# Cached attention and a gated MLP in one decode kernel: each 8 MB pair loaded as two halves, one from SyncE's queue and one from ScalarE's

## The chip, the cores and the metric

The kernel runs on one core of a Trainium2 chip. The metric is the device time of one execution in microseconds, the median of the runs shown. A core has five engines with a queue of instructions each: TensorE (PE in the profile, its weight loads PEld), VectorE (DVE), ScalarE (ACT), GpSimd (POOL) and SyncE (SP). Transfers between HBM and the on-chip memory (SBUF) are issued by an engine's queue and carried out by 16 DMA engines, which belong to none of these.

## The reference

For four sequences with one new token each, the result is `g * a + (1 - g) * b`, where `g` is a sigmoid gate.

```
g = sigmoid((x * gate_w).sum(-1, keepdims=True))         # x: 4 x 1 x 1024
# a: attention over a cache
q = (x @ wq) as 32 heads of 128                          # wq: 1024 x 4096
p = softmax(q . k_cache * 128 ** -0.5)                   # k_cache: 4 x 32 x 8192 x 128
a = (p . v_cache) as 4096 columns @ wo                   # v_cache: the same; wo: 4096 x 1024
# b: an MLP (with one token per sequence the choice by w_r chooses that token)
r = x @ w_r
b = x + sigmoid(r) * ((silu(x @ w_gate) * (x @ w_up)) @ w_down)   # F = 3584
```

All inputs are bf16. The caches are 268 MB each; every byte of them is used once, for one query. All inputs together are 576 MB.

## The kernel before

**Pairs.** A cache is worked through in 32 *pairs*. Pair `d` holds four heads of one sequence: 128 partitions (4 heads x 32) with 64 KB each, 8.39 MB. The constant `RING` is half of that per partition (16384 elements, 32 KB), and `UN` is a quarter (16 KB, over all partitions 2 MB): a *unit*. The weights `wq`, `w_gate` and `w_up` come as one pair each, too (`w_gate` and `w_up` with 56 KB per partition), and `w_down` takes the room of a pair.

**The ring.** All of this lands in one SBUF tile, `flat` ("ring" in the profile), with room for `NU` = 11 units. A list written out by hand, `plan`, gives for every load in turn the unit where it begins and the order in which its four units are used (UP: first to last, DOWN: last to first). A pair whose place is 8 or more does not fit in one piece: its second half lies elsewhere (from unit 0, for the last pair from unit 2). The new pair takes up to three units that are free already, and one or more that the pair in use has just given back.

**Loads.** `load_pair` (L194 to L209) issues the load of a pair on SyncE's queue. Where the pair lies in one piece it is a single DMA with rows of 64 KB (L204); where it does not, or where `cuts` asks for it, it is cut (L209). It is called where the pair's use begins: in `wq_piece`'s place (wq), in `gu_piece` (gate and up), in `k_pair` and in `v_pair`. SyncE's instructions are kept in an order that is not written by hand (`manual_schedule` lists PE, DVE and Pool alone), but it issues nearly nothing but these loads, one after the other. Before each it waits on semaphores until PE has done its last matmul on the units that the load overwrites. The wait is for all units of one DMA together.

**Work on K (`k_pair`).** A unit is turned by two transposes of DVE in place (L511, 128x2048 words each), and each of these is followed by 8 matmuls of PE into the scores `S_ps` (L516). After the eighth pair of a group of eight come maximum, exp (on ScalarE, L545) and a transpose of the weights into `PT`.

**Work on V (`v_pair`).** PE multiplies the weights spread out in `PB` with the units, 16 matmuls per unit (L587) into `o_ps`. ScalarE and GpSimd spread `PT` into `PB` (L568, L570); after every second pair `sum_up` folds `o_ps` into `OS` (ScalarE L613, DVE L617), and `finish` brings that into the heads' output.

**Order.** V runs eight pairs (`LAG`) behind K: wq, gate, K0, K1, up, K2 to K8, V0, K9, V1 and so on to K31, then w_down, V23, and the last eight V pairs. `w_down` (`wd_piece`) is loaded and used between K31 and V23. `wo` (`wo_two`, `wo_block`) comes around and behind the last V pair, in pieces that grow smaller, and ends the kernel: its matmuls (L296), a copy and two small stores, one from SyncE and one from ScalarE, which is the only transfer on ScalarE's queue.

**Start.** `begin_early` moves SyncE's first DMA (the load of wq) ahead of the start barrier. After it SyncE issues three small loads of `x`, `w_r` and `gate_w` (L228 to L230).

Of the kernel before, what the change touches and what calls it, by code (L numbers as in the profile page):

```python
# [112 lines left out]
def kernel(  # L113
# [15 lines left out]
    nc = tc.nc  # L129
    P = 128  # L130
    Bn, Sq, D = A_x.shape
    _, H, Sk, Dh = A_k_cache.shape
    F = B_w_gate.shape[1]
    DT = D // P
    NQ = 4
    QP = P // NQ
    JR = Sk // QP // 2
    CJ = 64
    JT = JR // CJ
    RD = 2 * JT  # L140
    GD = QP // RD
    GH = GD * NQ
    ND = Bn * H // NQ
    LAG = GD
# [8 lines left out]
    RING = JR * Dh  # L153
    UN = RING // 2
# [10 lines left out]
    accp = ctx.enter_context(tc.tile_pool(name="accp", bufs=1, space=PSUM))  # L165
    scores = ctx.enter_context(ExitStack())
    scp = scores.enter_context(tc.tile_pool(name="scp", bufs=1, space=PSUM))
    ctx.enter_context(tc.manual_schedule(engines={mybir.EngineType.PE, mybir.EngineType.DVE, mybir.EngineType.Pool}))
    nc.at_finalize(keep_weights)
    nc.at_finalize(drop_implied)  # L170
    nc.at_finalize(begin_early)
# [19 lines left out]
        tb_turn[0] += 1  # L191
        return t[lo:lo + rows, 0:n] if dtype == BF else t[lo:lo + rows, 0:2 * n].bitcast(dtype)

    def load_pair(src, n, cuts=(1, 1), second=None):  # L194

        place, down = next(plan)
        lo = place * UN
        if second is None:
            second = place * UN + n if place + 4 <= NU else 0
        at = [lo, second]  # L200
        assert second or (n == RING and lo + n == NU * UN and not down)
        halves = [flat[:, x:x + n] for x in at]
        if cuts == (1, 1) and second == lo + n:
            nc.sync.dma_start(out=flat[:, lo:lo + 2 * n], in_=src)  # L204
        else:
            for i, half in enumerate(halves):
                step = n // cuts[i]
                for x in range(0, n, step):
                    nc.sync.dma_start(out=half[:, x:x + step], in_=src[:, i * n + x:i * n + x + step])  # L209
        return halves, list(range(RD))[::-1] if down else list(range(RD))  # L210


    S0 = scp.tile([P, 4, NB], F32, name="S_ps")
# [8 lines left out]
        return b[:, 0:n].rearrange("p (%s) -> p %s" % (" ".join(names), " ".join(names)), **dict(zip(names, shape)))  # L222

    N = H * Dh
    wq_at, _ = load_pair(A_wq.rearrange("(c t) n -> c (t n)", t=DT), DT // 2 * N)
    NX = Bn + 2
    x6 = const.tile([NX, D], BF)
    nc.sync.dma_start(out=x6[0:Bn], in_=x2)  # L228
    nc.sync.dma_start(out=x6[Bn:Bn + 1], in_=B_w_r.rearrange("(o n) -> o n", o=1))
    nc.sync.dma_start(out=x6[Bn + 1:Bn + 2], in_=gate_w.rearrange("(o n) -> o n", o=1))  # L230


    q_ps = S0[:, 0:2]
# [61 lines left out]
    def mm_acc(n, lhsT, rhs, start=False):  # L295
        nc.tensor.matmul(acc(n), lhsT=lhsT, rhs=rhs, start=start, stop=True, skip_group_check=True)  # L296
# [20 lines left out]
            mm_acc(n, dg[:], xf[:, n * NB:(n + 1) * NB])  # L317


    TW = DT // 2  # L320


    FI = FG * FR - 1
    FB = P * FI
    SX = 5
# [19 lines left out]

    def wq_piece():
        x_rows(q_ps, wq_at, N // NB, lambda w, t, i: [(0, FR, w[:, t * N + i * NB:t * N + (i + 1) * NB])])

    def q_done():
        qs = turned(P, 8 * P).rearrange("p (z c d) -> p z c d", z=2, c=4)  # L350
# [10 lines left out]
                             start=True, stop=True)  # L361
        nc.vector.tensor_copy(out=qa[:].rearrange("p e h b -> p e (h b)"), in_=qa_ps)

    def gu_piece(view, w_i):

        ws, _ = load_pair(view.rearrange("(c t) f -> c (t f)", t=DT), TW * F)

        def cols(w, t, i):
            row = w[:, t * F:t * F + FB].rearrange("p (f m) -> p f m", m=FI)
            if i < FG - 1:  # L370
                return [(0, FR, row[:, :, FR * i:FR * i + FR])]
            return [(0, FR - 1, row[:, :, FR * i:FI]), (FR - 1, FR, w[:, t * F + FB:(t + 1) * F])]
        x_rows(o_ps[w_i], ws, FG, cols)

    def h_done():
        h = turned(P, 1024, F32).rearrange("p (z n) -> p z n", z=2)
# [24 lines left out]
            nc.gpsimd.tensor_copy(out=cS[lo:lo + m, 0:n], in_=c12[lo:lo + m, 1:2, :].to_broadcast([m, n, Bn]))  # L401
        nc.vector.tensor_tensor(out=hS[:], in0=hs_ps[0:72], in1=cS[:], op=ALU.mult)

    def wd_piece():
        lo = next(plan)[0] * UN
        assert (FI + SX) * D == 2 * RING and lo + 2 * RING <= NU * UN
        w = flat[:, lo:lo + 2 * RING]
        at = FI * D
        nc.sync.dma_start(out=w[:, 0:at], in_=wdv)
        for u in range(2):  # L410
            nc.sync.dma_start(out=w[32 * u:32 * u + 12, at:at + SX * D], in_=wd_apart[u])
        nc.sync.dma_start(out=w[64:72, at:at + D], in_=wd_rest)
        parts = [(hT[:, i // FR, i % FR, :], w[:, i * D:(i + 1) * D]) for i in range(FI)]
        parts += [(hS[:, v, :], w[0:72, at + v * D:at + (v + 1) * D]) for v in range(SX)]
        for i, (lhsT, rows) in enumerate(parts):
            for n in range(NH):
                mm_acc(n, lhsT, rows[:, n * NB:(n + 1) * NB], start=(i == 0))

    WB = P * FR // Dh
    NWB = H // WB  # L420
# [55 lines left out]
    def flush_late():  # L476
        while late:
            late.pop(0)()

    def heads(d):  # L480
        return divmod(d * NQ, H)

    def kv_view(cache, d):
        b, h0 = heads(d)
        return cache[b, h0:h0 + NQ].rearrange("h (r j) d -> (h r) (j d)", j=2 * JR)

    def spread(d):
        b, h0 = heads(d)
        Z = Zt[d % 2]
# [4 lines left out]
    def k_pair(d):  # L494
        g, t = divmod(d, GD)
        Z = Zt[d % 2]
        if d == 0:
            spread(0)
        if t == 0:
            S_ps[g] = S0  # L500
        sps = S_ps[g]
        ks, order = load_pair(kv_view(A_k_cache, d), RING)
        flush_sums()
        for k, n in enumerate(order):
            unit = ks[n // JT][:, (n % JT) * UN:(n % JT + 1) * UN]
            kn = unit.bitcast(U32).rearrange("p (j h i) -> p h j i", j=CJ, h=2)
            T = unit.rearrange("p (j h i e) -> p h j i e", j=CJ, h=2, e=2)
            s = QP - 1 - (RD * t + n)
            for half in range(2):
                step = 2 * k + half  # L510
                nc.vector.transpose(out=kn[:, half], in_=kn[:, half])  # L511
                if step < 2 and ahead:
                    ahead.pop(0)()
                for e in range(2):
                    for z in range(4):
                        nc.tensor.matmul(sps[:, z, :], lhsT=Z[:, 2 * half + e, s:s + P], rhs=T[:, half, 16 * z:16 * z + 16, :, e],  # L516
                                         start=(t + k + half + e == 0),
                                         stop=(t == GD - 1 and k == RD - 1 and half + e == 2))
                if step == RD and d + 1 < ND:
                    spread(d + 1)  # L520
                if step == RD:
                    flush()
                if step == RD + 2:
                    flush_late()
        if t == GD - 1:
            ahead.extend(softmax(g))
            while g > 0 and ahead:
                ahead.pop(0)()
# [45 lines left out]
    def v_pair(d):  # L574
        b, h0 = heads(d)
        g, t = divmod(d, GD)
        tv = t % GV
        row = NM * tv
        flush_sums()
        vv = kv_view(A_v_cache, d)  # L580
        vs, order = load_pair(vv, RING, {ND - 2: (1, 2), ND - 1: (2, 2)}.get(d, (1, 1)), 2 * UN if d == ND - 1 else None)
        for u in range(4 * RD):
            n, z = order[u // 4], u % 4
            vn = vs[n // JT]
            for w in range(4):
                j0 = CJ * (n % JT) + 16 * z + 4 * w
                nc.tensor.matmul(o_ps[w // 2][row:row + NM, w % 2, :],  # L587
                                 lhsT=PB[:, RD * (d % NW) + n, z].rearrange("p w s j -> p (w s j)"),
                                 rhs=vn[:, j0 * Dh:(j0 + 4) * Dh], start=(u == 0), stop=(u == 4 * RD - 1),
                                 skip_group_check=True)  # L590
            if u == 1:
                flush()
            if u == 7:
                flush_late()
        if tv == GV - 1:
            sum_up(d, g, t, b, h0)

        if g == NG - 1:
            if t < 2:
                spread_p(d + NW)  # L600
            if t == 3:
                spread_p(d + NW - 1, 2)
        elif t == NW - 1:
            spread_p(d + 1, NW)
        elif t == GD - 1:
            if g + 1 < NG - 1:
                spread_p(d + 1, NW)
            else:
                spread_p(d + NW)
# [41 lines left out]
    wq_piece()  # L651
    q_done()
    gates()
    gu_piece(B_w_gate, 0)
    side = {1: lambda: (gu_piece(B_w_up, 1), h_done())}
    GE = NWB - HV // WB
    order = []
    for d in range(ND):
# [2 lines left out]
    for kind, d in order:  # L661
        if kind == "k":
            k_pair(d)
            if d in side:
                side[d]()
            if d == ND - 1:
                scores.close()
                fin = ctx.enter_context(tc.tile_pool(name="fin", bufs=1, space=PSUM))
                A_ps.extend(fin.tile([P, NB], F32, name=f"acc{n}") for n in range(NH))
                A_ps.append(fin.tile([P, 2, NB], F32, name="led"))  # L670
                wd_piece()
                add_x()
        if (kind, d) == ("v", ND - 1):
            first, second = wo_two(0)
            first()
            last = [second]
        if kind == "v":
            v_pair(d)
        if (kind, d) == ("v", ND - 2):
            o_rows(0, GE)  # L680
# [47 lines left out]
```

## Time and profile before

| | us |
|---|---|
| median of 3 runs (lowest, highest) | 1341.18 (1341.12, 1342.13) |
| the profiled execution | 1340.96 |
| its span, first to last instruction | 1339.2 |
| PE busy | 1031.3 (77%) |
| DVE busy | 638.7 (48%) |
| POOL busy | 67.0 (5%) |
| ACT busy | 57.7 (4%) |

The page states the busy time of each engine, digits for 40 slices of the span, the DMA queues with what they moved, the chain of work that ended last, and the groups of instructions by line. In the DMA rows a packet is one contiguous row that one DMA engine moves; q1 is SyncE's queue, q10 ScalarE's, q8 and q14 fetch instructions and tables. In the chain in order of time a row has its start, its duration and the work; for a DMA the duration runs from its issue to its landing. In the waits of SyncE's queue a row has who waited for whom, the total in us, how often, and the longest.

### The profile page before, as it was taken

Reading aid. Unit: us, or ns where it says so; the run is one execution under the profiler, and the core shown is the slowest. Engines: PE = TensorE matmul, PEld = TensorE weight load, DVE = VectorE, ACT = ScalarE, POOL = GpSimd, SP = SyncE. Lnnn points to the kernel's source line nnn. Section 1 sums busy time; section 2 is a strip of 40 time slices with the busy share of each in tenths; the row PEclk is TensorE's granted clock in tenths of the full one; section 3 lists DMA queues with packets and bytes.
Section 4 is the critical chain, followed back from the end, with each engine's and each line's share of the span. In section 5 each row is a group of like instructions: output and inputs, shape, how many; then the busy total and the mean of one; then the engine's idle time right before and its main releaser. Section 6 shows DMA issues by size and latency. Waiting matters only on the chain.

```text
span 1339.2 us, 6936 instructions
## 1 busy us (share of the span) xinstructions
PE 1031.3 (77%) x4654; PEld 139.8 (10%) x1486; DVE 638.7 (48%) x385; ACT 57.7 (4%) x58; POOL 67.0 (5%) x174
## 2 busy tenths in 40 slices
PE   2386787887777788777787977777797778687887
PEld 0011000001010010101001110100111011111111
DVE  2285998556553436555352556634345556100001
ACT  0000000100010000100010000100000000110000
POOL 2000000100010000100010000100001000100000
PEclk9697998898888998888889988888998889689999
DMA  9999999999999999999999999999999999999998
GB/s 415 433 437 437 435 437 435 420 438 433 433 435 437 427 433 435 429 438 431 433 431 433 435 439 427 429 433 435 438 430 428 433 429 429 438 429 445 422 422 352
DMA packets 13032, 576.14 MB, mean 430 GB/s; under 512 B 1436, under 2 KB 1700, under 8 KB 1970
## 3 DMA queue, kind: packets, MB, share of 16 engines
q1 hardware_dynamic: 12994, 575.69, 99.6%
q8 instruction: 24, 0.39, 0.1%
q14 instruction: 6, 0.05, 0.0%
q10 hardware_dynamic: 8, 0.00, 0.0%
HBM read 575.68 MB, written 0.01 MB: 430 GB/s over the span
## 4 chain that ended last, share of the span: by engine, by line
DMA 67%; PE 22%; DVE 9%; POOL 0%; ACT 0%; issue 0%; SPq 0%
DMA ring<-in_A_k_cache_dram 53%; PE S_ps L516 15%; DMA ring<-in_A_v_cache_dram 10%; DVE ring L511 9%; PE o_ps L587 5%; DMA ring<-in_B_w_gate_dram 3%; DMA ring<-in_A_wo_dram 2%; PE o_ps L342 1%; POOL PB L570 0%; DVE mx L536 0%; PE led L633 0%; ACT TB L545 0%; PE acc L296 0%; POOL Z L492 0%; PE o_ps L633 0%
## 5 line engine op out<-in xcount | busy, mean ns | idle before, releaser
L511 DVE STREAM_TRANSPOSE ring<-ring 128x2048 uint32<-128x2048 uint32 x256 | 566.5, 2276 | 307.7 <-DMA ring<-in_A_k_cache_dram 307.7
L516 PE MATMUL S_ps<-ring,Z 128*128 128x512 bf16 x2048 | 519.9, 408 | 229.3 <-DVE ring L511 216.1
L587 PE MATMUL o_ps<-ring,PB 128*64 128x512 bf16 x2048 | 457.4, 384 | 35.7 <-DMA ring<-in_A_v_cache_dram 33.3
L516 PEld LDWEIGHTS <-Z 128*128 128x128 bf16 x512 | 53.0, 104 | 683.0 <-issue 683.0
L617 DVE SCALAR_TENSOR_TENSOR OS<-o_ps,mE,OS 128x512 f32<-128x512 f32 x33 | 24.8, 751 | 161.7 <-ACT OS L613 160.2
L587 PEld LDWEIGHTS <-PB 128*64 128x64 bf16 x512 | 56.7, 111 | 428.3 <-issue 427.6
L625 DVE SCALAR_TENSOR_TENSOR OS<-o_ps,mE,OS 128x512 f32<-128x512 f32 x5 | 3.7, 750 | 143.6 <-ACT OS L623 143.6
L492 POOL COPY Z<-qa 32x4 bf16<-32x4 bf16 x128 | 25.8, 201 | 716.7 <-PE S_ps L516 689.6
L570 POOL COPY PB<-PT 32x1024 bf16<-32x1024 bf16 (+3 forms) x23 | 33.4, 1452 | 466.6 <-PE o_ps L587 360.7
L613 ACT ACTIVATE OS<-o_ps,mE 128x512 f32<-128x512 f32 x11 | 7.6, 687 | 671.2 <-PE o_ps L587 671.2
L568 ACT COPY PB<-PT 32x1024 bf16<-32x1024 bf16 (+3 forms) x21 | 30.3, 1444 | 22.4 <-PE o_ps L587 17.4
L545 ACT ACTIVATE TB<-S_ps,mx 128x2048 bf16<-128x2048 f32 x4 | 7.9, 1967 | 321.7 <-DVE mx L542 321.7
L254 PE MATMUL S_ps<-identb,x 6*128 6x6 bf16 x8 | 0.6, 196 | 22.3 <-DMA x<-in_gate_w_dram 22.3
L342 PE MATMUL o_ps<-ring,xw 128*4 128x512 bf16 (+2 forms) x128 | 12.9, 490 | 3.5 <-DMA ring<-in_B_w_gate_dram 3.5
L633 PEld LDWEIGHTS o_ps<-selg,OS 128*128 128x128 f32 x88 | 11.5, 191 | 8.8 <-issue 8.5
L550 DVE STREAM_TRANSPOSE PT<-TB 128x2048 bf16<-128x2048 bf16 x4 | 9.2, 2312 | 6.4 <-ACT TB L545 6.4
L296 PE MATMUL acc<-ring,hT 128*4 128x512 bf16 x54 | 7.9, 466 | 5.5 <-DMA ring<-in_B_w_down_dram 5.5
L536 DVE TENSOR_REDUCE mx<-S_ps 128x1 f32<-128x2048 f32 x4 | 9.1, 2282 | 6.0 <-PE S_ps L516 6.0
L296 PE MATMUL acc<-ring,LT 128*4 128x512 bf16 x64 | 8.8, 378 | 3.3 <-DMA ring<-in_A_wo_dram 2.8
L633 PE MATMUL o_ps<-selg,OS 128*128 128x8 f32 x88 | 10.5, 245 | 0.0
L623 ACT ACTIVATE OS<-o_ps,mE 128x512 f32<-128x512 f32 x5 | 3.4, 687 | 151.2 <-PE o_ps L587 151.2
L256 DVE COPY xw<-S_ps 128x48 bf16<-128x48 bf16 x1 | 0.2, 184 | 17.5 <-PE S_ps L254 17.5
(83 smaller groups left out, 88.4 us busy)
## 6 DMA issues: line engine op xcount, KB each, us to landing
ring<-in_A_v_cache_dram SPq DMA_DIRECT2D x7, 4096.0 KB
ring<-in_A_k_cache_dram SPq DMA_DIRECT2D x6, 4096.0 KB, 33.9
ring<-in_A_v_cache_dram SPq DMA_DIRECT2D x6, 2048.0 KB, 28.9
ring<-in_B_w_gate_dram SPq DMA_DIRECT2D x1, 7168.0 KB
ring<-in_B_w_up_dram SPq DMA_DIRECT2D x1, 7168.0 KB
ring<-in_B_w_down_dram SPq DMA_DIRECT2D x1, 6912.0 KB
ring<-in_A_wo_dram SPq DMA_DIRECT2D x2, 2048.0 KB
ring<-in_A_wo_dram SPq DMA_DIRECT2D x3, 1024.0 KB, 34.5
```

What stands on the lines that cost most here:

```text
L296: nc.tensor.matmul(acc(n), lhsT=lhsT, rhs=rhs, start=start, stop=True, skip_group_check=True)
L342: nc.tensor.matmul(ps[32 * k:32 * k + Bn, z, :].rearrange("p (f r) -> p f r", r=FR)[:, :, lo:hi], lhsT=xT[TW * half + t], rhs=rhs, start=( ...
L492: nc.gpsimd.tensor_copy(out=Z[at, :, QP - 1 + QP * q], in_=qa[at, :, h0 + q, b])
L511: nc.vector.transpose(out=kn[:, half], in_=kn[:, half])
L516: nc.tensor.matmul(sps[:, z, :], lhsT=Z[:, 2 * half + e, s:s + P], rhs=T[:, half, 16 * z:16 * z + 16, :, e], start=(t + k + half + e == 0) ...
L536: nc.vector.tensor_reduce(out=mx[:, 0:1], in_=sps[:].rearrange("p z n -> p (z n)"), axis=AX.X, op=ALU.max)
L550: nc.vector.transpose(out=PT[:].rearrange("p j i -> p (j i)"), in_=PTs)
L568: nc.scalar.copy(out=Bv[at, :, :, q, :], in_=Pv[at])
L570: nc.gpsimd.tensor_copy(out=Bv[at, :, :, q, :], in_=Pv[at])
L587: nc.tensor.matmul(o_ps[w // 2][row:row + NM, w % 2, :], lhsT=PB[:, RD * (d % NW) + n, z].rearrange("p w s j -> p (w s j)"), rhs=vn[:, j0 ...
L617: nc.vector.scalar_tensor_tensor(out=OS[:], in0=o_ps[w // 2][:, w % 2, :], scalar=mE[:, w:w + 1], in1=OS[:], op0=ALU.mult, op1=ALU.add)
L633: nc.tensor.matmul(oT, lhsT=OS[:, q * Dh:(q + 1) * Dh], rhs=selg[:, q].rearrange("p t s -> p (t s)"), start=(q == 0), stop=(q == 3), skip_ ...
```

## The change

`load_pair` is replaced by a list of loads and a function that issues from it:

- `queue` enters a load into `stream`, with its place, its order of use and its four units; all loads are entered at the beginning, in the order of before and with the same places.
- `pump` issues the loads at the head of the list as long as all units of the next one are free at that point of the program (`held`). A load with `cuts == (1, 1)`, which is each but the last two V pairs, is issued as two DMAs with half of each row: the first half from SyncE, the second from ScalarE. This holds for the pairs that lie in one piece as well. `wd_load` cuts the large part of `w_down` in the same way.
- `take` gives a load's halves to the work that begins, and `let_go` marks units as free behind the last matmul that reads them, unit by unit in `k_pair` and `v_pair`, and calls `pump`.
- The order of ScalarE's and SyncE's instructions is now that of the program (`manual_schedule` lists both).

Work, places, orders of use and the loads of `wo` stay as they were. The core of the diff:

```diff
-    ctx.enter_context(tc.manual_schedule(engines={mybir.EngineType.PE, mybir.EngineType.DVE, mybir.EngineType.Pool}))
+    ctx.enter_context(tc.manual_schedule(engines={mybir.EngineType.PE, mybir.EngineType.DVE, mybir.EngineType.Pool, mybir.EngineType.Activation, mybir.EngineType.SP}))
-    def load_pair(src, n, cuts=(1, 1), second=None):
+    def queue(name, src, n, cuts=(1, 1), second=None):
         place, down = next(plan)
         lo = place * UN
         if second is None:
             second = place * UN + n if place + 4 <= NU else 0
-        at = [lo, second]
+        units = [place, place + 1, second // UN if second != lo + n else place + 2]
+        units.append(units[2] + 1)
-        halves = [flat[:, x:x + n] for x in at]
-        if cuts == (1, 1) and second == lo + n:
-            nc.sync.dma_start(out=flat[:, lo:lo + 2 * n], in_=src)
-        else:
+        stream.append((name, src, n, cuts, lo, second, down, units))
+
+    def pump(want=None):
+        while stream:
...
+            name, src, n, cuts, lo, second, down, units = stream[0]
+            if any(held[u] is not None for u in units):
+                break
+            stream.pop(0)
+            halves = [flat[:, x:x + n] for x in (lo, second)]
             for i, half in enumerate(halves):
                 step = n // cuts[i]
+                q = nc.scalar if i and cuts == (1, 1) else nc.sync
                 for x in range(0, n, step):
-                    nc.sync.dma_start(out=half[:, x:x + step], in_=src[:, i * n + x:i * n + x + step])
+                    q.dma_start(out=half[:, x:x + step], in_=src[:, i * n + x:i * n + x + step])
+            for u in units:
+                held[u] = name
+            loaded[name] = (halves, units, list(range(RD))[::-1] if down else list(range(RD)))
+
+    def take(name):
+        pump(name)
+        return loaded[name]
+
+    def let_go(name, k=None):
+        for u in loaded[name][1] if k is None else [loaded[name][1][k]]:
+            held[u] = None
+        pump()
...
+    fit("gate", B_w_gate)
+    for d in range(ND):
+        queue(("k", d), kv_view(A_k_cache, d), RING)
+        if d == 1:
+            fit("up", B_w_up)
+        if d == ND - 1:
+            stream.append(("down", next(plan)))
+        if d >= LAG and d - LAG < ND - LAG:
+            queue(("v", d - LAG), kv_view(A_v_cache, d - LAG), RING)
+    for d in range(ND - LAG, ND):
+        if d == ND - 1:
+            stream.append(("wo", wo_places[0] // 2))
+        queue(("v", d), kv_view(A_v_cache, d), RING, {ND - 2: (1, 2), ND - 1: (2, 2)}.get(d, (1, 1)), 2 * UN if d == ND - 1 else None)
+    pump()
...
-        nc.sync.dma_start(out=w[:, 0:at], in_=wdv)
+        nc.sync.dma_start(out=w[:, 0:at // 2], in_=wdv[:, 0:at // 2])
+        nc.scalar.dma_start(out=w[:, at // 2:at], in_=wdv[:, at // 2:at])
...
-        ks, order = load_pair(kv_view(A_k_cache, d), RING)
+        ks, _, order = take(("k", d))
...
+            let_go(("k", d), n)
...
-        vs, order = load_pair(vv, RING, {ND - 2: (1, 2), ND - 1: (2, 2)}.get(d, (1, 1)), 2 * UN if d == ND - 1 else None)
+        vs, _, order = take(("v", d))
...
+            if z == 3:
+                let_go(("v", d), n)
```

More of the change, by code (lines that the diff above doesn't have):

```diff
@@ L192, in turned @@
         return t[lo:lo + rows, 0:n] if dtype == BF else t[lo:lo + rows, 0:2 * n].bitcast(dtype)
-    def load_pair(src, n, cuts=(1, 1), second=None):
+    stream = []
+    loaded = {}
+    held = [None] * NU
+    def queue(name, src, n, cuts=(1, 1), second=None):
         place, down = next(plan)
@@ L199, in load_pair @@
             second = place * UN + n if place + 4 <= NU else 0
-        at = [lo, second]
+        units = [place, place + 1, second // UN if second != lo + n else place + 2]
+        units.append(units[2] + 1)
         assert second or (n == RING and lo + n == NU * UN and not down)
-        halves = [flat[:, x:x + n] for x in at]
-        if cuts == (1, 1) and second == lo + n:
-            nc.sync.dma_start(out=flat[:, lo:lo + 2 * n], in_=src)
-        else:
+        stream.append((name, src, n, cuts, lo, second, down, units))
+    def pump(want=None):
+        while stream:
+            if stream[0][0] == "wo":
+                if held[stream[0][1]] is not None:
+                    break
+                held[stream.pop(0)[1]] = "wo"
+                loaded["wo"] = wo_two(0)
+                continue
+            if stream[0][0] == "down":
+                units = [stream[0][1][0] + u for u in range(4)]
+                if any(held[u] is not None for u in units):
+                    break
+                wd_load(stream.pop(0)[1])
+                for u in units:
+                    held[u] = "down"
+                continue
+            name, src, n, cuts, lo, second, down, units = stream[0]
+            if any(held[u] is not None for u in units):
+                break
+            stream.pop(0)
+            halves = [flat[:, x:x + n] for x in (lo, second)]
             for i, half in enumerate(halves):
                 step = n // cuts[i]
+                q = nc.scalar if i and cuts == (1, 1) else nc.sync
                 for x in range(0, n, step):
-                    nc.sync.dma_start(out=half[:, x:x + step], in_=src[:, i * n + x:i * n + x + step])
-        return halves, list(range(RD))[::-1] if down else list(range(RD))
+                    q.dma_start(out=half[:, x:x + step], in_=src[:, i * n + x:i * n + x + step])
+            for u in units:
+                held[u] = name
+            loaded[name] = (halves, units, list(range(RD))[::-1] if down else list(range(RD)))
+        assert want is None or want in loaded, (want, stream[0][0], held)
+    def take(name):
[5 more added lines that the diff above has]
+        pump()
     S0 = scp.tile([P, 4, NB], F32, name="S_ps")
@@ L224 @@
     N = H * Dh
-    wq_at, _ = load_pair(A_wq.rearrange("(c t) n -> c (t n)", t=DT), DT // 2 * N)
+    TW = DT // 2
+    queue("wq", A_wq.rearrange("(c t) n -> c (t n)", t=DT), TW * N)
+    wq_at, _, _ = take("wq")
     NX = Bn + 2
@@ L230, with kv_view, fit @@
     nc.sync.dma_start(out=x6[Bn + 1:Bn + 2], in_=gate_w.rearrange("(o n) -> o n", o=1))
+    def kv_view(cache, d):
+        b, h0 = divmod(d * NQ, H)
+        return cache[b, h0:h0 + NQ].rearrange("h (r j) d -> (h r) (j d)", j=2 * JR)
+    def fit(name, view):
+        queue(name, view.rearrange("(c t) f -> c (t f)", t=DT), TW * F)
+    fit("gate", B_w_gate)
[12 more added lines that the diff above has]
+    pump()
     q_ps = S0[:, 0:2]
@@ L317, in add_x @@
             mm_acc(n, dg[:], xf[:, n * NB:(n + 1) * NB])
-    TW = DT // 2
     FI = FG * FR - 1
@@ L347, in wq_piece @@
         x_rows(q_ps, wq_at, N // NB, lambda w, t, i: [(0, FR, w[:, t * N + i * NB:t * N + (i + 1) * NB])])
+        let_go("wq")
     def q_done():
@@ L362, in q_done, with gu_piece @@
         nc.vector.tensor_copy(out=qa[:].rearrange("p e h b -> p e (h b)"), in_=qa_ps)
-    def gu_piece(view, w_i):
-        ws, _ = load_pair(view.rearrange("(c t) f -> c (t f)", t=DT), TW * F)
+    def gu_piece(name, w_i):
+        ws, _, _ = take(name)
         def cols(w, t, i):
@@ L373, in gu_piece @@
         x_rows(o_ps[w_i], ws, FG, cols)
+        let_go(name)
     def h_done():
@@ L402, in h_done, with wd_load @@
         nc.vector.tensor_tensor(out=hS[:], in0=hs_ps[0:72], in1=cS[:], op=ALU.mult)
-    def wd_piece():
-        lo = next(plan)[0] * UN
+    def wd_load(place):
+        lo = place[0] * UN
         assert (FI + SX) * D == 2 * RING and lo + 2 * RING <= NU * UN
@@ L412, in wd_piece @@
         nc.sync.dma_start(out=w[64:72, at:at + D], in_=wd_rest)
+        loaded["down"] = (w, [place[0] + u for u in range(4)], None)
+    def wd_piece():
+        w, at = take("down")[0], FI * D
         parts = [(hT[:, i // FR, i % FR, :], w[:, i * D:(i + 1) * D]) for i in range(FI)]
@@ L417, in wd_piece @@
                 mm_acc(n, lhsT, rows[:, n * NB:(n + 1) * NB], start=(i == 0))
+        let_go("down")
     WB = P * FR // Dh
@@ L481, in heads @@
         return divmod(d * NQ, H)
-    def kv_view(cache, d):
-        b, h0 = heads(d)
-        return cache[b, h0:h0 + NQ].rearrange("h (r j) d -> (h r) (j d)", j=2 * JR)
     def spread(d):
@@ L579, in v_pair @@
         flush_sums()
-        vv = kv_view(A_v_cache, d)
-        vs, order = load_pair(vv, RING, {ND - 2: (1, 2), ND - 1: (2, 2)}.get(d, (1, 1)), 2 * UN if d == ND - 1 else None)
+        vs, _, order = take(("v", d))
         for u in range(4 * RD):
@@ L653 @@
     gates()
-    gu_piece(B_w_gate, 0)
-    side = {1: lambda: (gu_piece(B_w_up, 1), h_done())}
+    gu_piece("gate", 0)
+    side = {1: lambda: (gu_piece("up", 1), h_done())}
     GE = NWB - HV // WB
@@ L673 @@
         if (kind, d) == ("v", ND - 1):
-            first, second = wo_two(0)
+            first, second = take("wo")
             first()
```

## The prediction

> **What bounds the kernel now.** I read the page's DMA rows first, because the kernel reads half a gigabyte and computes little with it, then the chain of waits as a share by engine, then the chain in order of time, and last SyncE's own queue.
>
> ```profile
> DMA  9999999999999999999999999999999999999998
> DMA packets 13032, 576.14 MB, mean 430 GB/s; under 512 B 1436, under 2 KB 1700, under 8 KB 1970
> q1 hardware_dynamic: 12994, 575.69, 99.6%
> q8 instruction: 24, 0.39, 0.1%
> DMA 67%; PE 22%; DVE 9%; POOL 0%; ACT 0%; issue 0%; SPq 0%
> ```
>
> The reader is to see that SyncE's queue (q1) alone keeps the 16 DMA engines in use for 99.6% of the span. PE and DVE stand on the chain only because a load is released by them; from release to landing there is room, as the next lines show.
>
> ```profile
> 245.18 24.91 DMA ring<-in_A_k_cache_dram
> ...
> 280.98 27.88 DMA ring<-in_A_k_cache_dram
> ...
> 320.64 26.94 DMA ring<-in_A_k_cache_dram
> ...
> 358.78 27.50 DMA ring<-in_A_k_cache_dram
> ...
> 398.60 26.38 DMA ring<-in_A_k_cache_dram
> ```
>
> These are issues of K pairs and the time to their landing. The landings, start plus duration, are 270.09, 308.86, 347.58, 386.28 and 424.98: every 38.7 us one K pair and one V pair, 16.78 MB, so 433.5 GB/s, and one pair (8.39 MB) is 19.35 us of transfer. A load takes 24.9 to 27.9 us to land, so it lies 5.5 to 8.5 us in the queue behind the load before it: the queue never runs dry.
>
> ```profile
> 572.87 0.33 SPq L204 DMA_DIRECT2D ring<-in_A_v_cache_dram  x1
> 593.39 0.33 SPq L204 DMA_DIRECT2D ring<-in_A_k_cache_dram  x1
> SPq L204 <- PE S_ps L516: 572.6, 29, 26.2
> SPq L204 <- PE o_ps L587: 430.0, 24, 24.8
> ```
>
> SyncE holds nothing but loads. It stands before the next one, waiting for PE's last read of a ring unit, for a thousand of 1339 us. Loads are thus already issued the moment their last unit is given back.
>
> From the first byte (about 1 us) to 1335 us the kernel is a stream of DMA packets; what follows is 4 us of tail. So the time is: bytes, divided by the rate of a packet, plus what breaks the stream.
>
> **The change, part by part.** The profiled execution took 1340.96 us (span 1339.2, so 1.8 around it), 0.2 below the median 1341.18; I make the sum on the former and add 0.2.
>
> *Halves instead of wholes.* Before, 57 pairs (wq, 29 K, 27 V) come as one DMA with rows of 64 KB; gate and up have 56 KB rows, down 54 KB. Each row is one packet on one engine. Now all of these come as two rows half as long. The other pairs (six that wrap round the ring's end, and the last two) already come in 32 KB rows or less and keep them. Each engine carries 8 rows of a DMA, so the change adds 57 x 8 + 2 x 8 + 8 = 480 packets per engine. The bytes are the same. The trace records every packet (these records stand behind the DMA rows of the page): undisturbed ones of 64 KB took 2421.65 ns on average (433.0 GB/s over 16 engines), those of 32 KB 1216.71 ns (430.9), and they follow one another without a gap. Two of the short ones take 11.8 ns more than a long one, so 480 x 11.8 ns = 5.6 us. The chain gives a second price: between 270.09 and 308.86 lies V pair 1, which wraps and so comes as two halves: 38.77 us, where the next two intervals take 38.72 and 38.70. That is 0.06 us per divided pair, and 60 of them make 3.6 us.
>
> *More DMAs.* 60 further DMAs, each with a 4-byte completion packet of 9 ns per engine (1437 such records before, 16 per DMA): 60 x 9 ns = 0.5 us.
>
> The two prices of this part are 5.6 + 0.5 = 6.1 us (records) and 3.6 us (chain, which contains the completion packets); I take 5.0, between them. This is on the path: the engines have no idle time to hide it.
>
> *Two queues instead of one.* 66 halves go to ScalarE's queue (q10), which before carried only the last output. Then each engine serves two rings in turn. No row of before shows two loaded rings, so I bound it. Below: with the next packet of the other ring ready, the 11.8 ns gap could vanish, for these halves and for the six wrapped pairs: (960 + 96) packets x 11.8 ns = 12.4 us off the new stream. Above: the only change of ring in the trace is an instruction fetch (q8, 16 KB). Around the one at 494.6 us its engine lost 1018 ns to the fetch and 547 ns in the next 64 KB packet, 1.57 us for what is 0.61 us as a 16 KB packet of q1: 0.48 us per change of ring. At every packet that would be 1056 x 0.48 = 507 us. These ends are far apart. The fetch is one lone packet into a ring that was empty, to another target; the nearest row for two full rings is that of packets that follow one another in a full ring, 11.8 ns apart, already in the price. So I take 0 on top. The Trainium skill ("DMA: Bandwidth & Descriptors", section "Issuing engines are not separate DMA queues") says the same of the direction: queues of different issuers end on the same 16 engines, and only issue time is saved. By it there is no gain in the second queue; the trace can't say yet.
>
> *Issue time.* An issue took 0.33 us on SyncE; 66 of them are 22 us on ScalarE's sequencer, beside 57.7 us of its own work in 1339. Cost nothing: cover is the 5.5 to 8.5 us that a load waits in the queue.
>
> *Who now stands behind whom on ScalarE.* Its queue is in program order: a half waits for PE to leave its two units, and behind it stand exp (L545 of before), the copies into PB (L568) and into OS (L613). Each of these needs a later point of the same PE order (the end of the pair whose units are being given back), so it loses nothing. The other way round, a half can stand behind one OS and two PB copies, 0.69 + 2 x 1.44 = 3.6 us after a V pair's end; the K half behind them needs units that PE gives back only after that. It has 5.5 us of cover at least: 0. If a half were later than that, the other ring still feeds the engines. On SyncE the first half no longer waits for the second's units, so it is in the queue sooner: 0 gain, since the queue is never dry.
>
> *Order of landing.* With both rings loaded they move at half rate each, so both halves of a pair land about when the whole did, 19.35 us after the pair before. The first one gains nothing, and DVE (18.3 us per K pair) starts as before.
>
> *Start and end.* wq's first half goes out before the start barrier as the whole did, and its 9.7 us cover the second half's later issue: 0. The three x loads stand behind 4 MB instead of 8 on SyncE's ring, at half the rate: about the 22.3 us of now. At the end the last two V pairs and wo stay on SyncE: 0.
>
> Sum: 1340.96 + 5.0 = 1346.0, against the median 1346.2 us (+0.37%). Its own range is 3.6 to 6.1 us: 1344.8 to 1347.3.
>
> **The rivals.** 0.2% (2.7 us) is about what a measurement can tell here.
>
> *The gap is hidden (faster).* Place: each engine's step from packet to packet. If two loaded rings overlap it, the 12.4 us come off 1346.2: 1333.8 us. It decides from 5.0 / 12.4 = 40% hidden. For it: the gap is constant (11.8 ns), like a fixed step that could be prepared beside a transfer. Against: inside one full ring, where the next packet is known just as early, it isn't hidden. The skill's page gives 435.2 GB/s as the ceiling of the ports (section "Where 436 GB/s comes from"); by it 576 MB take 1324 us, where the 433.0 of the 64 KB row makes 1330.6, so all that could be won is 6.7 us. The trace agrees: its best packets stay under that.
>
> *Part of it (no change).* About 40% hidden, or a gap far below 11.8 ns: 1341.2 us. The same page (section "Why small descriptors are slow (HBM only)") names about 3 cycles per packet; at its 850 MHz, an estimate of 3.5 ns, so 1.7 us: 1343. The rows say three times as much, and I go by them.
>
> *Changing rings costs (much slower).* If it costs one more gap per packet, 1346.2 + 12.4 = 1358.6; a twentieth of the fetch's price (24 ns) makes 1371. For it: the 0.96 us lost around each fetch although q1 was full. Against: the fetch's ring was empty.
>
> *ScalarE starves its ring.* A half behind exp that waits for DVE: four softmaxes, at most one pair each, 4 x 19.35 = 77 us: 1423 at worst. Against: what exp waits for comes before the next units are free.
>
> *"As soon as given back" does nothing.* SyncE's waits above say so; it is in my forecast.
>
> **How the numbers follow.** Forecast 0.5, hidden 0.2, part 0.15, change of rings 0.12, starving 0.03. Slower is 0.5 + 0.12 + 0.03 = 0.65, faster 0.2, same 0.15. The range reaches from the hidden gap, 1333.8, to one more gap per packet, 1358.6; beyond it lie most of the ring changes and the starving, about 0.13.
>
> **What would show it.** Right: q10 with some 275 MB (66 halves), q1 with 300; a mean rate near 428 GB/s; K landings every 38.8 to 38.95 us; no 64 KB packets; DMA still at 9 throughout; PE, DVE and tail unchanged. Wrong: landings below 38.7 us (hidden gap); above 39.2 (changing rings costs); slices with DMA under 9, with ScalarE's waits before a load (starving).

## The result and the profile after

The changed kernel took 1345.63 us (median of 7 runs, 1345.52 to 1346.38), the kernel before 1341.14 us (7 runs, 1340.95 to 1342.13): a ratio of 1.0034, 95% interval 1.0023 to 1.0046, so slower by 4.5 us. The prediction was 1346.2 us. The profiled execution took 1345.52 us with a span of 1343.7.

The DMA rows of the page after and the shares of its chain, to be held against the first view of the prediction:

```profile
DMA  9999999999999999999999999999999999999998
DMA packets 21672, 576.14 MB, mean 429 GB/s; under 512 B 2396, under 2 KB 2660, under 8 KB 2930
q1 hardware_dynamic: 12130, 300.57, 52.1%
q10 hardware_dynamic: 9512, 275.13, 47.6%
q8 instruction: 24, 0.39, 0.1%
DMA 64%; PE 20%; DVE 15%; issue 0%; ACT 0%; another core or an unknown queue 0%; SPq 0%
```

The engines are as full as before (52.1 and 47.6 make 99.7%) and move the same 576.14 MB. What grew is the number of packets, by 8640: 7680 data packets (480 on each of 16 engines) and 960 of 4 bytes that report a DMA's end (60 DMAs, 16 each). The rate over the span sinks from 430 to 429 GB/s.

The chain of waits of after, in order of time, for a DMA with its issue and its duration to landing:

```profile
312.16 9.97 PE S_ps L582 x32
322.13 0.02 issue
322.15 29.02 DMA ring<-in_A_k_cache_dram
...
363.34 24.27 DMA ring<-in_A_k_cache_dram
...
398.65 29.02 DMA ring<-in_A_k_cache_dram
...
439.14 26.18 DMA ring<-in_A_k_cache_dram
...
476.75 30.17 DMA ring<-in_A_k_cache_dram
```

These landings are 351.17, 387.61, 427.67, 465.32 and 506.92. The intervals swing between 36.4 and 41.6 us where before each was 38.7; their mean is 38.94. The two rings do move in step, but not together: the last completion packets of SyncE's halves came at 387.0, 406.4 and 425.9 us and those of ScalarE's at 388.4, 407.8 and 427.2, each every 19.4 us and 1.4 apart (2.6 apart around 350 us). A pair used in order UP begins with SyncE's half, one used DOWN with ScalarE's, so that the start of work moves to and fro. It costs nothing, since the engines stay full: DVE's transposes waited 314.7 us for K loads, before 307.7.

The halves of a pair are issued at different times, because each waits for its own units. These are the K halves in the timeline of after, SyncE's (SPq) and ScalarE's (ACTq):

```profile
304.51 0.33 SPq L235 DMA_DIRECT2D ring<-in_A_k_cache_dram  x1
322.15 0.33 ACTq L235 DMA_DIRECT2D ring<-in_A_k_cache_dram  x1
340.96 0.46 ACTq L235 DMA_DIRECT2D ring<-in_A_k_cache_dram  x1
363.34 0.33 SPq L235 DMA_DIRECT2D ring<-in_A_k_cache_dram  x1
```

In the second of these pairs ScalarE's half was issued 22.4 us before SyncE's and landed 1.4 us after it (388.4 and 387.0). With both rings full, an earlier issue is only a longer wait in the ring.

ScalarE was not held up, nor did it hold up its loads: the load at 322.15 was issued 0.02 us after PE's matmuls ended, as the first lines of the chain show, and so were those at 398.65 and 476.75. These are two waits of ScalarE (ACT) and one each of DVE and PE, after, in the view of who waited for whom:

```profile
ACT OS L681 <- PE o_ps L653: 672.4, 11, 79.6
ACT PB L635 <- PE o_ps L653: 18.9, 1, 18.9
DVE ring L577 <- DMA ring<-in_A_k_cache_dram: 314.7, 31, 23.8
PE S_ps L319 <- DMA x<-in_gate_w_dram: 25.2, 1, 25.2
```

The first two were 671.2 and 17.4 us before. The end is unchanged: the last packet of a load (of `wo`) ended at 1335.50 us before and at 1339.88 now, 4.4 us later, and from there to the end of the span it is 3.7 us before and 3.8 now.

### The profile page after: what moved, and what is told of

Its sections match the earlier page's. It is cut to its first block, busy times and chain, and to the rows that moved or that the text cites. A ratio compares the mean times of both kernels' runs of the same rounds, so it can differ in the third digit from the quotient of the medians.

```text
span 1343.7 us, 6997 instructions
## 1 busy us (share of the span) xinstructions
PE 1039.9 (77%) x4654; PEld 143.1 (11%) x1486; DVE 638.6 (48%) x385; ACT 57.7 (4%) x58; POOL 66.6 (5%) x174
## 2 busy tenths in 40 slices
DMA packets 21672, 576.14 MB, mean 429 GB/s; under 512 B 2396, under 2 KB 2660, under 8 KB 2930
## 3 DMA queue, kind: packets, MB, share of 16 engines
q1 hardware_dynamic: 12130, 300.57, 52.1%
q10 hardware_dynamic: 9512, 275.13, 47.6%
## 4 chain that ended last, share of the span: by engine, by line
DMA 64%; PE 20%; DVE 15%; issue 0%; ACT 0%; another core or an unknown queue 0%; SPq 0%
DMA ring<-in_A_k_cache_dram 49%; DVE ring L577 14%; DMA ring<-in_A_v_cache_dram 11%; PE S_ps L582 11%; PE o_ps L653 8%; DMA ring<-in_B_w_gate_dram 3%; DMA ring<-in_A_wo_dram 2%; PE o_ps L404 1%; PE acc L361 1%; DVE mx L603 0%; DVE PT L617 0%; ACT TB L612 0%; PE led L701 0%; PE o_ps L701 0%
## 5 line engine op out<-in xcount | busy, mean ns | idle before, releaser
L577 DVE STREAM_TRANSPOSE ring<-ring 128x2048 uint32<-128x2048 uint32 x256 | 566.4, 2275 | 314.7 <-DMA ring<-in_A_k_cache_dram 314.7
L319 PE MATMUL S_ps<-identb,x 6*128 6x6 bf16 x8 | 0.6, 196 | 25.2 <-DMA x<-in_gate_w_dram 25.2
```

## The experiments

Two theories were to be told apart. *Packet length*: rows of 32 KB instead of 64 KB have a fixed step more often. *Two queues*: the engines' change between two rings, or the loads in ScalarE's order, costs the time. A third question was whether the rest of the change does anything. For this the packet records were read more closely than in the prediction: each packet was matched by time with the one that starts as it ends, which is taken to be the next on the same engine, and the step is the time from start to start. It is 2418.1 ns for 64 KB and 1213.2 for 32 KB before, and 1213.4 after.

**e1: halves, one queue.** The kernel before, each pair cut:

```diff
-        if cuts == (1, 1) and second == lo + n:
+        if False:
             nc.sync.dma_start(out=flat[:, lo:lo + 2 * n], in_=src)
         else:
...
-        nc.sync.dma_start(out=w[:, 0:at], in_=wdv)
+        for x in range(0, at, at // 2):
+            nc.sync.dma_start(out=w[:, x:x + at // 2], in_=wdv[:, x:x + at // 2])
```

> The kernel before with one edit: every pair, and the large part of w_down, is issued as two halves one behind the other on SyncE's queue alone. Theory (packet length): the trace of after shows packets starting 1213.3 ns apart for 32 KB and 1213.4 on ScalarE's queue, that of before 2418.1 ns for 64 KB; two short ones are 8.5 ns dearer, 480 more of them per engine make 4.1 us, 60 more completion packets 0.4 us: 1345.6 us, the same as after, with one queue. Rival (two queues): if the loss came from the engines changing between two rings or from the new order of ScalarE's queue, this kernel stays at 1341.1 us.

Measured: 1346.27 us (1345.67 to 1346.48), ratio 1.0034, interval 1.0022 to 1.0046. The DMA rows of its page:

```profile
DMA packets 21672, 576.14 MB, mean 429 GB/s; under 512 B 2396, under 2 KB 2660, under 8 KB 2930
q1 hardware_dynamic: 21634, 575.69, 99.7%
```

As many packets as after, nearly all in SyncE's queue, with a step of 1213.3 ns, and the same loss. The second queue is not needed for it, and it takes nothing off it.

**e3: quarters, two queues.** The kernel after, each half issued as two DMAs with 16 KB rows:

```diff
-                step = n // cuts[i]
+                step = n // (2 if cuts == (1, 1) else cuts[i])
```

> The kernel after with each half cut once more, into two DMAs with rows of 16 KB on the same queue. A dose for the packet length: 1056 packets per engine of 32 KB (480 pairs of them from the division and 96 of the wrapped pairs) become 2112 of 16 KB. In the trace of before packets of 16 KB start 611.2 ns apart, those of 32 KB 1213.2: two are 9.2 ns dearer than one. So 1056 x 9.2 ns = 9.7 us and 132 more completion packets x 5.9 ns = 0.8 us on top of after: 1356.1 us. Rival (two queues): the rings are two as before, so 1345.6 us.

Measured: 1355.61 us (1355.56 to 1356.26), ratio 1.0106, interval 1.0093 to 1.0119. The step of a 16 KB packet was 610.8 ns in SyncE's ring and 611.4 in ScalarE's, so two are 8.8 ns dearer than one of 32 KB. With the same two rings the loss follows the number of packets.

**e6: the list of loads, whole pairs, one queue.** The kernel after without its two queues and halves:

```diff
...
-                q = nc.scalar if i and cuts == (1, 1) else nc.sync
...
+            if cuts == (1, 1) and second == lo + n:
+                nc.sync.dma_start(out=flat[:, lo:lo + 2 * n], in_=src)
+            else:
...
+                    q = nc.sync
...
-        nc.sync.dma_start(out=w[:, 0:at // 2], in_=wdv[:, 0:at // 2])
-        nc.scalar.dma_start(out=w[:, at // 2:at], in_=wdv[:, at // 2:at])
+        nc.sync.dma_start(out=w[:, 0:at], in_=wdv)
```

> The kernel after with the pairs as in the kernel before: one DMA with 64 KB rows where a pair lies in one piece, and SyncE alone. What stays of the change is the list of loads, the issue where the units are given back and the order of SyncE's and ScalarE's instructions by hand. Theory (this part does nothing, SyncE was waiting for its units already): 1341.2 us. Rival (earlier issue is worth something, and after hid a part of its loss with it): below 1339 us.

Measured: 1341.13 us (1340.94 to 1342.28), beside 1341.01 for the kernel before; ratio 1.0002, interval 0.9993 to 1.0011. Its packets count 13032, as before. Issuing from a list when units are given back, with the order by hand, is worth nothing here.

**e2: halves by partitions, two queues.** An attempt to have both halves at once and keep the 64 KB rows. The kernel after, but for a pair in one piece (and w_down alike):

```diff
...
+                for q, p in ((nc.sync, 0), (nc.scalar, P // 2)):
+                    q.dma_start(out=flat[p:p + P // 2, lo:lo + 2 * n], in_=src[p:p + P // 2])
...
```

> The kernel after with one edit: a pair that lies in one piece is halved by partitions (0 to 63 from SyncE, 64 to 127 from ScalarE), so the rows stay 64 KB long; wrapped pairs as in after. Theory (packet length): two queues in lock step, as many data packets as before, 60 more completion packets per pair of rings but each engine still gets one per DMA, 0.4 us: 1341.5 us. Rival (two queues): 1345.6 us. A third outcome: 64 partitions over 16 engines send all engines to half of the partitions at a time; if the landing side minds that, packets take longer than 2422 ns and the time is well above 1346 us.

Measured: 2516.27 us (2404.71 to 2543.97); the profiled execution took 2537.38. The third outcome came. Its DMA rows:

```profile
DMA  9999999999999999999989999999999998998997
DMA packets 13992, 576.14 MB, mean 227 GB/s; under 512 B 2396, under 2 KB 2660, under 8 KB 2930
q1 hardware_dynamic: 8290, 300.57, 50.5%
q10 hardware_dynamic: 5672, 275.13, 48.0%
```

The engines are in use all the time and move half as much: a packet of 64 KB took 4807 ns on average, before 2425. The 32 KB packets of the wrapped pairs, which go to all 128 partitions, kept about their step in the median (1217 to 1218 ns, before 1213); their mean is longer, and the likely reason, not followed up, is that many of them shared the stream with halved pairs.

**e7: halves by partitions, one queue.** To see whether two rings have a part in that, the kernel before with

```diff
-            nc.sync.dma_start(out=flat[:, lo:lo + 2 * n], in_=src)
+            for p in (0, P // 2):
+                nc.sync.dma_start(out=flat[p:p + P // 2, lo:lo + 2 * n], in_=src[p:p + P // 2])
```

> The kernel before with each pair that lies in one piece cut by partitions, 0 to 63 and then 64 to 127, both on SyncE's queue; w_down stays whole. Tells whether e2 was slow from its partitions or from two rings. Theory (the partitions written at a time): packets near 4800 ns and a time near 2500 us with one queue too. Rival (two rings with such DMAs): 1341.5 us. In one queue all engines go through the lower half and then the upper half, so about all 57 pairs and three weights should pay: 57 pairs x 19.35 us more and 2 x 17 us, 2480 us.

Measured: 2593.66 us in one run, beside the 2480 expected; its 64 KB packets took 5044 ns on average. One queue suffices, so e2 says nothing against two. It shows that DMAs which fill 64 neighbouring partitions from 64 neighbouring rows run at half the rate.

**e5: even and odd partitions, two queues.** The kernel of e2 with this edit, and w_down alike:

```diff
-                for q, p in ((nc.sync, 0), (nc.scalar, P // 2)):
-                    q.dma_start(out=flat[p:p + P // 2, lo:lo + 2 * n], in_=src[p:p + P // 2])
+                for q, p in ((nc.sync, 0), (nc.scalar, 1)):
+                    q.dma_start(out=flat[p:P:2, lo:lo + 2 * n], in_=src[p:P:2])
```

> The kernel of e2 with one edit: the halves are the even partitions (SyncE) and the odd ones (ScalarE), so each DMA again has 64 rows of 64 KB but they lie over all of the 128 partitions. Theory (packet length, and in e2 the partitions written at a time): packets back at 2422 ns, as many data packets as before, 0.4 us for more completion packets: 1341.5 us, with two queues in lock step. Rival (two queues, or DMAs of 64 rows, are slow as such): packets near 4802 ns as in e2 and about 2500 us, or at least 1345.6 us as in after.

Measured: 2387.42 us (2379.55 to 2396.22), ratio 1.7802, interval 1.7774 to 1.7831. As a time it missed, and for a reason that was not foreseen. Its DMA rows, and two of its waits:

```profile
DMA  9636455465454545454456655364536465484999
q1 hardware_dynamic: 8290, 300.57, 30.8%
q10 hardware_dynamic: 5672, 275.13, 26.8%
DVE ring L581 <- DMA ring<-in_A_k_cache_dram: 725.0, 28, 47.6
DVE ring L581 <- DMA ring<-in_A_v_cache_dram: 552.0, 22, 37.1
```

The engines stood idle for much of the time: a K pair's transposes now waited for a V load too, so that loads and work took turns. The likely cause, not tried apart, is that the waits derived for a region with a step over partitions cover the other units as well. But while loads were under way, the engines served the two rings in turn, packet by packet, with 64 KB rows, and their step was 2417.5 ns in SyncE's ring and 2415.3 in ScalarE's, within 3 ns of the 2418.1 of one ring before. (Left out is the first packet of an engine after it stood idle: some 3.1 us.) So a change of ring costs nothing that can be seen, and it hides no more than these 3 ns. It also shows that a DMA of 64 rows is not slow as such.

**e4: whole pairs, by turns from two queues.** The kernel after with the edit below; the large part of w_down is one DMA from SyncE.

```diff
...
+            if cuts == (1, 1) and second == lo + n:
+                turn.append(name)
+                q = nc.scalar if len(turn) % 2 == 0 else nc.sync
+                q.dma_start(out=flat[:, lo:lo + 2 * n], in_=src)
+            else:
...
```

> The kernel after with one edit: a pair that lies in one piece is one DMA with 64 KB rows again, issued by turns from SyncE and from ScalarE; wrapped pairs as in after. No short packets, so by packet length alone 1341.2 us. But here two rings carry two different pairs, and while both are loaded each gets half the rate: the pair that is needed next lands late by up to 9.7 us while the ring has no room for a third pair. Theory (what matters of two queues is whether both carry the same pair): the queue runs dry at times, DMA under 9 in some slices, 1355 to 1370 us. Rival: the units are given back early enough all the same, 1341 to 1343 us.

Measured: 1375.43 us (1366.63 to 1378.65), ratio 1.0243, interval 1.0221 to 1.0266. The direction was right, the size 5 us beyond the range given. Two stretches of e4 and, in the second fence, the same of after (start and end in us, length, busy time of PE, PEld, DVE, ACT and POOL with their instructions, granted clock, DMA share, GB/s):

```profile
30.00:60.00 30.00, 14.47 (x164) 4.82 (x101) 4.78 (x13) 0.18 (x1) 2.25 (x8) 0.94 0.73 305
320.00:350.00 30.00, 18.89 (x84) 3.05 (x28) 18.60 (x11) 0.00 (x0) 0.79 (x4) 0.78 0.88 368
```

```profile
30.00:60.00 30.00, 11.85 (x124) 3.87 (x73) 3.94 (x9) 1.46 (x2) 2.24 (x8) 0.75 1.01 433
320.00:350.00 30.00, 24.02 (x116) 4.01 (x37) 7.95 (x6) 0.00 (x0) 0.78 (x4) 0.98 1.00 430
```

In e4 wq and gate arrive together at half rate each (wq's landing took 37.0 us, before 21.8), so that neither frees its units early, and the engines have nothing to do for 8 us; that happens again, more mildly, later on (2.9 us around 335). Before the tail the engines' idle time adds up to 23 us (after: 0.5). Some 10 us more lie in packets that took longer than usual; what lengthened those was not followed up.

## Why the prediction was right

The mechanism was the forecast's: the engines are full, a division of the rows adds 480 packets to each, and nothing else in the change is on the path. By its steps:

- *Halves instead of wholes.* Shown by e1 and e3. The first price was too high: it was taken from how long packets take (2421.65 and 1216.71 ns, a difference of 11.8 ns), but packets on one engine overlap by some 3.5 ns, more often so when there are more of them. The step from start to start is the right measure, 2 x 1213.36 - 2418.07 = 8.65 ns. With it the 480 packets make 4.1 us instead of 5.6. The second price, 3.6 us from the chain, was too low: it rests on 0.06 us per pair, read from landings that differ by 0.02 us among themselves, where the steps make it 8 x 8.65 + 5.9 = 75 ns. One price lay 1.6 us above the measured 4.5 and the other 0.9 below; that 5.0, chosen between them, came near is in part luck.
- *More DMAs.* 60 completion packets with a step of 5.9 ns, 0.35 us instead of 0.5. The two terms then make 4.5 us, which is what was measured. The interval of the measured ratio reaches from 3.1 to 6.2 us, so it is the packets' steps and not the times that tell the prices apart.
- *Two queues instead of one*, taken as 0: right. One ring (e1) and two (after) have the same step. The upper end of 0.48 us per change of ring, taken from the instruction fetch, says nothing of two full rings: it was not approached.
- *Issue time, ScalarE's order, start and end*, taken as 0: right as to time. The x loads landed at 25.2 us, 2.9 later than said, without consequence: the DMA digits stay at 9.
- *Order of landing.* Here the prediction was wrong in detail: both halves were to land about when the whole did, and K landings every 38.8 to 38.95 us. That is true of the mean alone (38.94); one by one they swing by 5 us. The signs that were named for the rivals, landings below 38.7 or above 39.2 us apart, are thus met by single intervals of after, though neither rival came true. Only the mean of several, or the packets' steps, could decide.

Of the rivals, *the gap is hidden* and *changing rings costs* fall by the steps of after and of e5: in 32 KB packets two rings have one ring's step to 0.1 ns (1213.4 and 1213.3, e1), in 64 KB packets to 3 ns. *Part of it* falls with them, and by the measured 4.5 us. The Trainium skill ("DMA: Bandwidth & Descriptors", section "Why small descriptors are slow (HBM only)") names about 3 cycles per packet, by the prediction's estimate 3.5 ns. The traces do not agree: here it was 8.65 to 8.8 ns. *ScalarE starves its ring* falls by the DMA digits, 9 throughout. That *as soon as given back* does nothing is shown by e6 (ratio 1.0002).

## What to carry to other kernels

Where the DMA rows show the engines full in every slice, count packets per engine before cutting a transfer: here each packet of 16 to 64 KB cost about 8.7 ns beside its bytes, whichever queue it came from, and a second queue neither cost nor gained anything. Measure such a price from start to start of neighbouring packets, not from their duration. If two queues are used for a stream of this kind, let them carry parts of the same load: in e4, where they carried two different loads, the one that was needed first arrived late, and the kernel took 34 us longer, 23 of them with the engines idle.

## What was not expected of the hardware

A DMA into 64 neighbouring partitions (0 to 63, or 64 to 127) had its 64 KB packets in 4807 ns (two queues) and 5044 ns (one queue), before 2425, although all engines were at work, while DMAs into every second partition kept 2421 once under way. The source rows lie next to each other or apart in the same way, so whether the reading or the writing side is the narrow one was not measured.

An instruction fetch of 16 KB cost its engine 1.57 us in the trace of before, where 16 KB in a full ring take 0.61. And ScalarE's first load, issued at 0.78 us, had its first packet at 5.2 us, while SyncE's, issued at 0, began at 1.0; SyncE's ring was full meanwhile, so it cost nothing. In the other runs with two queues this first packet came after whole packets of SyncE's ring, too: five per engine with 16 KB rows (e3, at 4.7 us), three with 32 KB (after), two with 64 KB (e4 and e5, at 6.5 and 6.8). So the wait grows with the rows of the other ring; its cause stays open.
